# Pooled scores on four quarters of the PE array, and a pair of transposes in one go

## The chip, the cores and the metric

The kernel runs on one core of a Trainium2 chip. The metric is the device time of one execution in microseconds. The kernel before took 961.01 us (median of three runs, 960.36 to 964.61). Of an execution recorded by the hardware profiler there is a trace, and all rows below come from it.

## The reference

Two attentions are added, and the sum goes through a two-layer network. Shapes are fixed: batch 8, 8 heads, 576 positions, head dimension 64, so 4608 tokens of 512 features, and a hidden width of 2048.

```python
q_d, k_d, v_d = (a.reshape(B, H, 144, 4, D).mean(axis=3) for a in (q, k, v))   # pooled by 4
out_up = np.repeat(sm_attn(q_d, k_d, v_d), 4, axis=2)      # softmax attention, 144 x 144 scores a head
scores = where(abs(i - j) < 4, q @ k.T / 8, -1e9)          # local attention, 7 keys a query
out_local = softmax(scores) @ v
x = (out_up + out_local).transpose(0, 2, 1, 3).reshape(4608, 512)
h = x @ w_in
out = maximum(0.01 * h, h) @ w_out
```

(Shortened; both softmaxes subtract the maximum and divide by the sum plus 1e-9.)

## The kernel before, in words

The network is the bulk of PE's work. Its inputs are split into a high and a low part (`xh`, `xl`, weights and `gh`, `gl` likewise), and three products of parts make one. Tokens are worked off in 13 chunks of 256 to 384 columns; chunks 0 and 1 are batch 0, the others batches 1 to 7. For each chunk and each of 16 slices of the hidden width there is an up step (L706, 12 matmuls into a PSUM bank `hp`), an activation (L716, L717 on ACT, L719 on DVE: `gh`, `gl`, three buffers each) and a down step (L746, 12 matmuls into four banks `acc0` to `acc3`). `xh` and `xl` are double buffered by chunk.

The attention prepares x. For batches 1 to 7 the local part is multiplied on POOL (L567, L628) and summed on DVE (L573, L634). `landing` then transposes a piece of it on PE into a bank (L665), adds the widened pooled output (`up`, L652 and L672), and writes `xh` (L678) and `xl` (L680). A chunk's up steps wait for all its landings.

The pooled part is `pooled`, once for each batch and each pair of heads: four units in batch 0 at the start, 28 for the other batches. One unit: the loads of q and k (`qk`) and of v (`vs`); sums over four neighbours on DVE (L345; POOL does it for three of the four units of batch 0); scores on PE (L358): three query groups of 48, fetched as 64 columns, for each of the two heads, with head 0 on partitions 0 to 63 of the array and of the result and head 1 on 64 to 127, all in one bank; the maximum (L366) and its scaling (L367) on DVE; three exponentials with their sums on ACT (L370); the reciprocal on DVE (L373, L374), which frees the bank; the scaling (L382); the pooled v (L387); three transposes into a bank and their copy, twice (L397 on PE, L399 on ACT); the product with v (L409) and its copy to `outd` (L414).

PSUM has eight banks: four `acc`, two `hp`, two `pt`. Until the first chunk is ready, batch 0 may take any of them (`banks`). After that the scores, the transposes and products of `pooled` and the transposes of `landing` share the two `pt` banks.

The order of all instructions is planned when the program is built. Each step is a generator that asks for buffers (`slot`), waits for events and puts operations with an estimated duration (`op`, `pe`, `load`); `Order.run` always takes the operation that can start first by these estimates, and among equals the one of lower rank. Engines work off their queues in the order so written. A holder of a `pt` bank is moved up in rank (`HURRY`). A wait on a bank is thus planned around by the estimate, and held by a semaphore on the chip. All loads are issued on SP's queue.

Of the kernel before, what the change touches and what calls it, by code (L numbers as in the profile page):

```python
# [6 lines left out]
F32 = mybir.dt.float32  # L7
# [6 lines left out]
AF = mybir.ActivationFunctionType  # L14
ALU = mybir.AluOpType
AX = mybir.AxisListType
# [3 lines left out]
FAC = 4  # L20
SD = S // FAC
# [5 lines left out]
SCALE = 1.0 / D ** 0.5  # L27
MAXSEG = 4
SIZES = (4, 5, 6, 6, 6, 6, 6, 6, 6, 6, 6)
QB = 48  # L30
# [6 lines left out]
HEADS = 2  # L37
# [145 lines left out]
def attn_moe(ctx: ExitStack, tc, qkt, vd, qb, kb, vb, vwb, band, identb, w_in, w_out, ident, edge, out):  # L183
    nc = tc.nc

    const = ctx.enter_context(tc.tile_pool(name="const", bufs=1))
    wk = ctx.enter_context(tc.tile_pool(name="wk", bufs=1))
    ps = ctx.enter_context(tc.tile_pool(name="ps", bufs=1, space=PSUM))

    bufs = dict(head=HEADS, qk=1, vs=1, qk_d=2, v_d=1, su_vd=2, su_half=1, su_pd=3, su_ptd=2, st_d=3, pd=2, ptd=1, outd=2, q=1, k=1, v=1, s=3, st_l=3, prod=2, up=1,  # L190
                xloc=2, lst=3, gh=3, gl=3, o=2, hp=2, pt=2, xh0=1, xl0=1, xh1=1, xl1=1, acc0=1, acc1=1, acc2=1, acc3=1,
                su_vw=NC, su_vs=NC, su_pt=2)
    od = Order(bufs)
# [1 line left out]
    def slot(*tags):  # L195
        return (yield ("slot", tags, 0))

    def sb(s, shape, dtype, pool=None):
        tag = s.tag
        return (pool or wk).tile(shape, dtype, name=tag, tag=tag, bufs=bufs[tag])  # L200

    def bank(s):
        return ps.tile([128, 512], F32, name=s.tag, tag=s.tag, bufs=bufs[s.tag])

    def op(eng, n, *after, times=1):
        if eng == "PE":
            dur = n
        else:
            a, k = COST[eng]
            dur = times * a + k * n  # L210
        return (yield ("op", eng, dur, max((0.0,) + after), 0, after))

    def pe(us, *after):
        return (yield ("op", "PE", us, max(after) + SAFE, 0))

    def load(out, in_, size, *after):
        t = yield ("op", "SP", 0.3, max((0.0,) + after), size)
        nc.sync.dma_start(out=out, in_=in_)  # L218
        return t

    def wait(name, n=1):
        return (yield ("wait", name, n))

    id_sb = const.tile([128, 128], F32, name="id_sb")
    edge_sb = const.tile([128, BLK, W], F32, name="edge_sb")
    w_in_v = w_in.rearrange("(c p) (f m) -> p f c m", p=128, m=128 * HALFS)
    w_out_v = w_out.rearrange("(f p) e -> p f e", p=128)
# [1 line left out]
    def fixed():  # L229
        yield from wait(("asked", 0, 0))  # L230
        for dst, src, name, size in ((idb_sb, identb, "idb", 32e3), (band_sb, band, "band", 160e3),
                                     (id_sb, ident, "id", 64e3)):
            od.signal(name, (yield from load(dst, src, size)))

    def edges():
# [51 lines left out]
    outd = {}  # L287
# [3 lines left out]
    def banks(b):  # L291
        return ("pt", "acc3", "acc2", "acc1", "acc0", "hp") if b == 0 and "started" not in od.events else ("pt",)
# [37 lines left out]
    def pooled(b, c, rank, pool=None):  # L330
        sq, sv, qk, vs, tq, tv = yield from fetch(b, c, pool)
        s_qd = yield from slot("qk_d")
        qk_d = sb(s_qd, [128, 2 * SD], F32)
        qkr = qk.rearrange("p a (s r) -> p (a s) r", r=FAC)
        if b < BANDED and (b, c) != (0, 0):
            s = yield from slot("su_half")
            half = sb(s, [128, 2 * SD, 2], F32, pool)
            t = yield from op("POOL", 576, tq, s.t, s_qd.t)
            nc.gpsimd.tensor_tensor(out=half, in0=qkr[:, :, :2], in1=qkr[:, :, 2:], op=ALU.add)
            t = yield from op("POOL", 288, t)  # L340
            nc.gpsimd.tensor_tensor(out=qk_d, in0=half[:, :, 0], in1=half[:, :, 1], op=ALU.add)
            s.free(t)
        else:
            t = yield from op("DVE", 1152, tq, s_qd.t)
            nc.vector.tensor_reduce(out=qk_d, in_=qkr, axis=AX.X, op=ALU.add)  # L345
        if sq:
            if b < BANDED:
                od.spawn(rank, keeper(b, c, sq, t))
            else:
                sq.free(t)  # L350
        s_st, s_pd = (yield from slot("st_d")), (yield from slot("su_pd" if pool else "pd"))
        s_b = yield from slot(*banks(b))
        sc = bank(s_b)
        t = yield from pe(0.9, t, s_b.t)
        for qi in range(3):
            for p in range(2):
                rows = slice(64 * p, 64 * p + 64)
                nc.tensor.matmul(sc[rows, qi * SD:(qi + 1) * SD], qk_d[rows, qi * QB:qi * QB + 64],  # L358
                                 qk_d[rows, SD:2 * SD], start=True, stop=True)
        s_qd.free(t)  # L360
        scv = sc[:, :3 * SD].rearrange("p (a s) -> p a s", a=3)
        st, pd = sb(s_st, [128, 2, 3], F32), sb(s_pd, [128, 3, SD], F32, pool)
        mx, rc = st[:, 0], st[:, 1]
        top, sm = sc[:, 3 * SD:3 * SD + 3], sc[:, 3 * SD + 4:3 * SD + 7]
        t = yield from op("DVE", 440, t, s_st.t, times=3)
        nc.vector.tensor_reduce(out=top, in_=scv, axis=AX.X, op=ALU.max)  # L366
        nc.vector.tensor_scalar(out=mx, in0=top, scalar1=-SCALE / (FAC * FAC), scalar2=None, op0=ALU.mult)  # L367
        t = yield from op("ACT", 432, t, s_pd.t, times=8)
        for qi in range(3):
            nc.scalar.activation(out=pd[:, qi], in_=scv[:, qi], func=AF.Exp, scale=SCALE / (FAC * FAC),  # L370
                                 bias=mx[:, qi:qi + 1], accum_out=sm[:, qi:qi + 1])
        t = yield from op("DVE", 10, t, times=4)
        nc.vector.tensor_scalar(out=rc, in0=sm, scalar1=1e-9, scalar2=float(FAC), op0=ALU.add, op1=ALU.mult)  # L373
        nc.vector.reciprocal(out=rc, in_=rc)  # L374
        s_b.free(t)
        if b < BANDED:
            t = yield from op("POOL", 432, t)
            nc.gpsimd.tensor_tensor(out=pd, in0=pd, in1=rc.unsqueeze(2).to_broadcast([128, 3, SD]), op=ALU.mult)
        else:
            t = yield from op("ACT", 432, t, times=5)  # L380
            for qi in range(3):
                nc.scalar.activation(out=pd[:, qi], in_=pd[:, qi], func=AF.Copy, scale=rc[:, qi:qi + 1])  # L382
        s_st.free(t)
        s_vd = yield from slot("su_vd" if pool else "v_d")
        v_d = sb(s_vd, [72, 2, 2, D], F32, pool)
        td = yield from op("DVE", 1050, tv, s_vd.t)
        nc.vector.tensor_reduce(out=v_d, in_=vs, axis=AX.X, op=ALU.add)  # L387
        if sv:
            sv.free(td)
        s_pt = yield from slot("su_ptd" if pool else "ptd")  # L390
        ptd = sb(s_pt, [72, 2, 2, 3, QB], F32, pool)
        for kc in range(2):
            s_b = yield from slot(*banks(b))
            tp = bank(s_b)
            tt = yield from pe(0.27, t, s_b.t)
            for qi in range(3):
                nc.tensor.transpose(tp[0:72, qi * 128:(qi + 1) * 128], pd[:, qi, kc * 72:kc * 72 + 72], id_sb)  # L397
            te = yield from op("ACT", 288, tt, s_pt.t)
            nc.scalar.copy(out=ptd[:, kc].rearrange("k p a q -> k a p q"),  # L399
                           in_=tp[0:72, :384].rearrange("k (a p q) -> k a p q", a=3, p=2)[:, :, :, :QB])  # L400
            s_b.free(te)
        s_pd.free(tt)
        to = yield from wait(("outd", b))
        s_b = yield from slot(*banks(b))
        av = bank(s_b)
        t = yield from pe(0.68, te, td, s_b.t)
        for p in range(2):
            for kc in range(2):
                nc.tensor.matmul(av[64 * p:64 * p + 64, :SD], v_d[:, p, kc], ptd[:, kc, p],  # L409
                                 start=kc == 0, stop=kc == 1)  # L410
        s_pt.free(t)
        s_vd.free(t)
        t = yield from op("ACT", 144, t, to)
        nc.scalar.copy(out=outd[b][:, c], in_=av[:, :SD])  # L414
        s_b.free(t)
        od.signal(("pooled", b, c), t)
        if b == 0:
            od.signal("su", t)
# [12 lines left out]
    def keeper(b, c, sq, t):  # L431
        sq.free(max(t, (yield from wait(("scored", b, c), 2))))
# [109 lines left out]
    VOFF, n = {}, 0  # L542
# [346 lines left out]
```

## Time and profile before

| | us |
|---|---|
| median of three runs (range) | 961.01 (960.36 to 964.61) |
| the profiled execution | 959.72 |
| its span, first to last instruction | 957.9 |
| PE busy | 932.4 |
| DVE, ACT, POOL busy | 595.2, 415.0, 617.8 |

The busy time of PE is a union of rows: matmuls are pipelined and overlap, so a row is longer than the step from one start to the next. The span is what the trace covers; the execution's own time is a little longer.

### The profile page before, as it was taken

What the parts mean: (1) busy time and instruction counts of PE and PEld (TensorE: products, weight loads), DVE (VectorE), ACT (ScalarE), POOL (GpSimd) and SP (SyncE); (2) the same over time, 40 slices, a digit from 0 to 9 for tenths busy, and PEclk for the clock granted to TensorE, in tenths of its full rate; (3) what the DMA queues carried; (4) which work ended last, traced back from release to release, by engine and by line L of the source; (5) the groups of instructions that cost most, each with busy time, mean ns of one, the idle gap of its engine ahead of it and who ended that gap; (6) DMA issues with size and microseconds to landing.
All of it is one profiled execution on the core that took longest, in us unless ns stands there. A gap on an engine that the chain in (4) does not pass through costs nothing.

```text
span 957.9 us, 16170 instructions
## 1 busy us (share of the span) xinstructions
PE 932.4 (97%) x6282; PEld 894.8 (93%) x6282; DVE 595.2 (62%) x895; ACT 415.0 (43%) x1139; POOL 617.8 (64%) x356
## 2 busy tenths in 40 slices
PE   6799999999999999999999999999999999999997
PEld 5588999899999999999999999899999999999997
DVE  5986678888887776787657774862753753311111
ACT  3774555555545543445324553532513423422211
POOL 3759868777888778986798776884885873100000
PEclk9899999999999999999999999999999999999999
DMA  9755665644554523452424442431231220000000
GB/s 264 241 184 181 214 201 179 189 164 145 188 166 122 190 96 116 131 187 95 135 74 146 159 148 101 140 116 58 92 116 58 91 77 31 34 1 1 34 1 33
DMA packets 63180, 117.31 MB, mean 122 GB/s; under 512 B 4944, under 2 KB 32848, under 8 KB 63104
## 3 DMA queue, kind: packets, MB, share of 16 engines
q1 hardware_dynamic: 63104, 116.29, 38.6%
q8 instruction: 49, 0.80, 0.4%
q14 instruction: 27, 0.22, 0.1%
HBM read 105.65 MB, written 10.62 MB: 121 GB/s over the span
## 4 chain that ended last, share of the span: by engine, by line
PE 77%; POOL 8%; DMA 4%; issue 4%; DVE 4%; ACT 2%; SPq 0%; POOLq 0%; DVEq 0%; ACTq 0%
PE hp L706 35%; PE acc L746 34%; POOL prod L567 4%; POOL prod L628 3%; PE pt L358 2%; DMA k<-in_kb_dram 2%; PE pt L397 2%; PE pt L409 2%; PE pt L665 1%; DMA qk<-in_qkt_dram 1%; DVE s L573 1%; DMA v<-in_w_in_dram 0%; SPq L218 0%; DMA vs<-in_w_out_dram 0%; DVE gl L719 0%
## 5 line engine op out<-in xcount | busy, mean ns | idle before, releaser
L567 POOL TENSOR_TENSOR prod<-q,k 128x1344 f32<-128x1344 f32 (+1 forms) x88 | 266.3, 3027 | 81.3 <-DMA k<-in_kb_dram 55.2
L628 POOL TENSOR_TENSOR prod<-v,s 128x1344 f32<-128x1344 f32 (+1 forms) x88 | 265.6, 3021 | 32.3 <-DVE xloc L634 18.2
L706 PE MATMUL hp<-xh,wih 128*128 128x384 f32 (+2 forms) x832 | 279.9, 336 | 5.8 <-DVE gl L719 5.1
L746 PE MATMUL acc<-gh,woh 128*128 128x384 f32 (+2 forms) x832 | 274.4, 330 | 0.3 <-ACT o L780 0.3
L706 PE MATMUL hp<-xl,wih 128*128 128x384 f32 (+2 forms) x832 | 269.5, 324 | 0.3 <-DVE xl L680 0.3
L706 PE MATMUL hp<-xh,wil 128*128 128x384 f32 (+2 forms) x832 | 269.6, 324 | 0.0
L746 PE MATMUL acc<-gh,wol 128*128 128x384 f32 (+2 forms) x832 | 269.0, 323 | 0.0
L746 PE MATMUL acc<-gl,woh 128*128 128x384 f32 (+2 forms) x832 | 268.9, 323 | 0.0
L719 DVE TENSOR_TENSOR gl<-hp,gh 128x384 fp32r<-128x384 f32 (+2 forms) x208 | 108.5, 522 | 215.7 <-ACT hp L717 215.2
L716 ACT ACTIVATE gh<-hp 128x384 fp32r<-128x384 f32 (+2 forms) x208 | 97.3, 468 | 315.6 <-PE acc L746 307.9
L706 PEld LDWEIGHTS hp<-xh,wih 128*128 128x128 f32 x832 | 156.4, 188 | 15.6 <-DVE gl L719 8.0
L746 PEld LDWEIGHTS acc<-gh,woh 128*128 128x128 f32 x832 | 156.2, 188 | 4.0 <-issue 3.2
L706 PEld LDWEIGHTS hp<-xl,wih 128*128 128x128 f32 x832 | 156.7, 188 | 0.5 <-DVE xl L680 0.5
L706 PEld LDWEIGHTS hp<-xh,wil 128*128 128x128 f32 x832 | 156.4, 188 | 0.0
L746 PEld LDWEIGHTS acc<-gl,woh 128*128 128x128 f32 x832 | 156.3, 188 | 0.0
L746 PEld LDWEIGHTS acc<-gh,wol 128*128 128x128 f32 x832 | 156.2, 188 | 0.0
L573 DVE TENSOR_REDUCE s<-prod 128x21 f32<-128x1344 f32 (+1 forms) x88 | 130.2, 1479 | 27.9 <-POOL prod L567 27.9
L634 DVE TENSOR_REDUCE xloc<-prod 128x192 f32<-128x1344 f32 (+1 forms) x88 | 130.1, 1478 | 22.5 <-POOL prod L628 22.1
L717 ACT ACTIVATE hp<-hp 128x384 f32<-128x384 f32 (+2 forms) x208 | 96.1, 462 | 0.0
L672 DVE TENSOR_TENSOR pt<-pt,up 128x384 f32<-128x384 f32 (+1 forms) x44 | 37.8, 861 | 27.6 <-PE pt L665 22.2
L652 ACT COPY up<-outd 128x576 f32<-128x576 f32 x84 | 52.3, 675 | 0.0
L370 ACT ACTIVATE pd<-pt,st_d 128x144 f32<-128x144 f32 x84 | 32.1, 382 | 46.4 <-DVE st_d L367 35.4
(154 smaller groups left out, 754.3 us busy)
## 6 DMA issues: line engine op xcount, KB each, us to landing
k<-in_kb_dram SPq DMA_DIRECT2D x38, 576.0 KB
v<-in_vb_dram SPq DMA_DIRECT2D x38, 576.0 KB
qk<-in_qkt_dram SPq DMA_DIRECT2D x32, 576.0 KB
vs<-in_vd_dram SPq DMA_DIRECT2D x28, 288.0 KB
q<-in_qb_dram SPq DMA_DIRECT2D x38, 192.0 KB
out_dram<-o SPq DMA_DIRECT2D x36, 192.0 KB
v<-in_w_out_dram SPq DMA_DIRECT2D x4, 512.0 KB
prod<-in_w_out_dram SPq DMA_DIRECT2D x4, 512.0 KB
```

Source lines behind the costliest of these rows:

```text
L370: nc.scalar.activation(out=pd[:, qi], in_=scv[:, qi], func=AF.Exp, scale=SCALE / (FAC * FAC), bias=mx[:, qi:qi + 1], accum_out=sm[:, qi:qi ...
L567: nc.gpsimd.tensor_tensor(out=prv, in0=q[:, p, a - j0:z - j0].unsqueeze(2).to_broadcast([128, n, W, D]), in1=view(k[:, p], (a - j0) * D, [ ...
L573: nc.vector.tensor_reduce(out=s[:, p, a - j0:z - j0], in_=prv, axis=AX.X, op=ALU.add)
L628: nc.gpsimd.tensor_tensor(out=prv, in0=view(v[:, p], a - j0, [[1, n], [nv, D], [1, W]]), in1=s[:, p, a - j0:z - j0].unsqueeze(2).to_broadc ...
L634: nc.vector.tensor_reduce(out=xl_t[:, :n, p], in_=prv, axis=AX.X, op=ALU.add)
L652: nc.scalar.copy(out=up[:, pp], in_=outd[b][:, 2 * u + pp].unsqueeze(2).to_broadcast([128, SD, FAC]))
L672: nc.vector.tensor_tensor(out=xv, in0=xv, in1=upv, op=ALU.add)
L706: nc.tensor.matmul(hp[:, :n], wt[:, c], x[:, c], start=k == 0, stop=k == 3 * NC - 1)
L716: nc.scalar.activation(out=gh[:, :n], in_=hp[:, :n], func=AF.Prelu, alpha=0.01)
L717: nc.scalar.activation(out=hp[:, :n], in_=hp[:, :n], func=AF.Prelu, alpha=0.01)
L719: nc.vector.tensor_tensor(out=gl[:, :n], in0=hp[:, :n], in1=gh[:, :n].bitcast(F32), op=ALU.subtract)
L746: nc.tensor.matmul(acc[:, :n], wt[:, es], g[:, :n], start=f == f0 and j == 0, stop=f == f1 - 1 and j == 2)
```

## The change: the diff

- The scores of query group 1 go to the other two quarters of the array: head 0 writes partitions 64 to 127 and head 1 partitions 0 to 63, into a second bank, `sx`. Groups 0 and 2 stay on the diagonal quarters and lie side by side in the first bank, `sc`.
- The heads of group 1 thus come out in swapped halves. The identity that transposes group 1 is turned to undo it: `id_sb` grows from 128 to 192 columns, and `turned[1]` is its columns 64 to 191.
- Both banks of a unit are asked for together, one unit at a time (`two`, a slot that is given back as soon as both are granted). The maximum becomes two instructions; the exponential of group 1 comes first, and `sx` is given back behind it.
- The six transposes of a unit follow one another into two banks that are held together; the two copies follow.
- The estimates for PE are 0.65 instead of 0.9 (scores) and 0.5 for all six transposes instead of 0.27 for each three.

```diff
-    id_sb = const.tile([128, 128], F32, name="id_sb")
+    id2_sb = const.tile([128, 192], F32, name="id_sb")
+    id_sb = id2_sb[:, :128]
+    turned = [id2_sb[:, 64 * n:64 * n + 128] for n in range(2)]
...
-                                     (id_sb, ident, "id", 64e3)):
+                                     (id2_sb, ident, "id", 96e3)):
...
+        s_two = yield from slot("two")
         s_b = yield from slot(*banks(b))
-        sc = bank(s_b)
-        t = yield from pe(0.9, t, s_b.t)
-        for qi in range(3):
-            for p in range(2):
-                rows = slice(64 * p, 64 * p + 64)
-                nc.tensor.matmul(sc[rows, qi * SD:(qi + 1) * SD], qk_d[rows, qi * QB:qi * QB + 64],
-                                 qk_d[rows, SD:2 * SD], start=True, stop=True)
+        s_x = yield from slot(*banks(b))
+        sc, sx = bank(s_b), bank(s_x)
+        s_two.free(0.0)
+        t = yield from pe(0.65, t, s_b.t, s_x.t)
+        for p, qi in ((0, 0), (1, 0), (0, 1), (1, 1), (0, 2), (1, 2)):
+            rows = slice(64 * p, 64 * p + 64)
+            h = 1 - p if qi == 1 else p
+            dst = sx[:, :SD] if qi == 1 else sc[:, qi // 2 * SD:(qi // 2 + 1) * SD]
+            nc.tensor.matmul(dst[64 * h:64 * h + 64], qk_d[rows, qi * QB:qi * QB + 64], qk_d[rows, SD:2 * SD], start=True, stop=True)
...
-        t = yield from op("DVE", 440, t, s_st.t, times=3)
-        nc.vector.tensor_reduce(out=top, in_=scv, axis=AX.X, op=ALU.max)
+        t = yield from op("DVE", 440, t, s_st.t, times=4)
+        nc.vector.tensor_reduce(out=top[:, 0:3:2], in_=sc[:, :2 * SD].rearrange("p (a s) -> p a s", a=2), axis=AX.X, op=ALU.max)
+        nc.vector.tensor_reduce(out=top[:, 1:2], in_=sx[:, :SD], axis=AX.X, op=ALU.max)
...
-        t = yield from op("ACT", 432, t, s_pd.t, times=8)
-        for qi in range(3):
-            nc.scalar.activation(out=pd[:, qi], in_=scv[:, qi], func=AF.Exp, ...
+        for n_, group in ((1, (1,)), (2, (0, 2))):
+            t = yield from op("ACT", 144 * n_, t, s_pd.t, times=2.7 * n_)
+            for qi in group:
+                nc.scalar.activation(out=pd[:, qi], in_=scs[qi], func=AF.Exp, ...
+            if n_ == 1:
+                s_x.free(t)
...
-        for kc in range(2):
-            s_b = yield from slot(*banks(b))
-            tp = bank(s_b)
-            tt = yield from pe(0.27, t, s_b.t)
+        s_two = yield from slot("two")
+        s_tp = [(yield from slot(*banks(b))), (yield from slot(*banks(b)))]
+        tps = [bank(x) for x in s_tp]
+        s_two.free(0.0)
+        tt = yield from pe(0.5, t, *(x.t for x in s_tp))
+        for kc, tp in enumerate(tps):
             for qi in range(3):
-                nc.tensor.transpose(tp[0:72, ...], pd[:, qi, kc * 72:kc * 72 + 72], id_sb)
-            te = yield from op("ACT", 288, tt, s_pt.t)
+                nc.tensor.transpose(tp[0:72, ...], pd[:, qi, kc * 72:kc * 72 + 72], turned[qi % 2])
+        te = s_pt.t
+        for kc, tp in enumerate(tps):
+            te = yield from op("ACT", 288, tt, te)
             nc.scalar.copy(out=ptd[:, kc] ...
```

## Rows read from the trace of the kernel before

**Rows 1.** The page's engines: busy time, share of the span, instructions.
```profile
PE 932.4 (97%) x6282; PEld 894.8 (93%) x6282; DVE 595.2 (62%) x895; ACT 415.0 (43%) x1139; POOL 617.8 (64%) x356
```
**Rows 2.** Stretches: length, busy (instructions) of each engine, PE clock, DMA share, GB/s.
```profile
372.00:450.00 78.00, 78.00 (x498) 74.04 (x497) 57.33 (x83) 34.94 (x104) 65.10 (x36) 1.00 0.45 145
```
**Rows 3.** PE's waits: releaser, us in total, times, longest.
```profile
PE hp L706 <- DVE gl L719: 5.1, 10, 1.4
```
**Rows 4.** Timeline around chunk 2's first up step: start, us, instruction, [idle before].
```profile
164.20 0.95 PE L358 MATMUL pt<-qk_d 64*64 64x144 f32 x12
...
167.74 0.18 DVE L374 RECIPROCAL st_d<-st_d 128x3 f32<-128x3 f32 x1
...
168.71 0.60 PE L665 MATMUL pt<-id_sb,xloc 128*128 128x128 f32 x4
...
170.77 0.38 PE L706 MATMUL hp<-xh,wih 128*128 128x256 f32 x1 [0.75 <-ACT xh L678]
```
**Rows 5.** Timeline where chunk 3's up steps begin.
```profile
224.91 0.41 DVE L680 TENSOR_TENSOR xl<-pt,xh 128x256 fp32r<-128x256 f32 x1
...
225.71 0.31 PE L706 MATMUL hp<-xh,wih 128*128 128x320 f32 x1
```
**Rows 6.** Timeline of DVE: the last `xl` of chunk 5.
```profile
352.63 0.56 DVE L680 TENSOR_TENSOR xl<-pt,xh 128x384 fp32r<-128x384 f32 x1
```
**Rows 7.** Timeline of PE: the first up step of chunk 5.
```profile
372.61 0.34 PE L706 MATMUL hp<-xh,wih 128*128 128x384 f32 x1
```
**Rows 8.** Stretches, L358 alone: length, busy (passes) of PE and of its loads.
```profile
100.00:169.00 69.00, 4.76 (x60) 3.42 (x60) 1.00 0.60 187
169.00:292.00 123.00, 8.57 (x108) 6.18 (x108) 1.00 0.52 166
292.00:640.00 348.00, 13.34 (x168) 9.58 (x168) 1.00 0.41 131
```
**Rows 9.** Timeline of PE around one block of scores.
```profile
119.09 0.28 PE L746 MATMUL acc<-gl,woh 128*128 128x256 f32 x1
119.21 0.28 PE L746 MATMUL acc<-gh,wol 128*128 128x256 f32 x1
119.42 0.95 PE L358 MATMUL pt<-qk_d 64*64 64x144 f32 x12
...
120.53 0.28 PE L706 MATMUL hp<-xl,wih 128*128 128x256 f32 x1
```
**Rows 10.** Timeline of PE: one block of the product with v.
```profile
305.23 0.72 PE L409 MATMUL pt<-ptd,v_d 72*64 72x144 f32 x8
```
**Rows 11.** Timeline of weight loads, 305.20 to 305.39 us: those begun by then.
```profile
305.23 0.20 PEld L409 LDWEIGHTS pt<-ptd,v_d 72*64 72x64 f32 x4 [0.25 <-issue]
```
**Rows 12.** Timeline of PE around one burst of pooled transposes.
```profile
307.47 0.34 PE L746 MATMUL acc<-gl,woh 128*128 128x384 f32 x1
307.65 0.33 PE L746 MATMUL acc<-gh,wol 128*128 128x384 f32 x1
307.82 0.49 PE L397 MATMUL pt<-id_sb,pd 128*72 128x128 f32 x3
...
308.32 0.34 PE L746 MATMUL acc<-gl,woh 128*128 128x384 f32 x1
```
**Rows 13.** Timeline of PE: two bursts of transposes back to back.
```profile
238.38 0.31 PE L746 MATMUL acc<-gl,woh 128*128 128x320 f32 x1
238.53 0.31 PE L746 MATMUL acc<-gh,wol 128*128 128x320 f32 x1
238.68 0.49 PE L397 MATMUL pt<-id_sb,pd 128*72 128x128 f32 x3
239.00 0.49 PE L665 MATMUL pt<-id_sb,xloc 128*128 128x128 f32 x3
...
239.48 0.30 PE L706 MATMUL hp<-xl,wih 128*128 128x320 f32 x1
```
**Rows 14.** Groups of DVE by form: count, busy us, mean ns, idle before.
```profile
L366 DVE TENSOR_REDUCE pt<-pt 128x3 f32<-128x432 f32 x28 | 17.2, 613 | 14.9 <-PE pt L358 14.8
```

More of the change, by code (lines that the diff above doesn't have):

```diff
@@ L188, in attn_moe @@
     ps = ctx.enter_context(tc.tile_pool(name="ps", bufs=1, space=PSUM))
-    bufs = dict(head=HEADS, qk=1, vs=1, qk_d=2, v_d=1, su_vd=2, su_half=1, su_pd=3, su_ptd=2, st_d=3, pd=2, ptd=1, outd=2, q=1, k=1, v=1, s=3, st_l=3, prod=2, up=1,
+    bufs = dict(head=HEADS, qk=1, vs=1, qk_d=2, v_d=1, su_vd=2, su_half=1, su_pd=3, su_ptd=2, st_d=3, pd=2, ptd=1, outd=2, q=1, k=1, v=1, s=3, st_l=3, two=1, prod=2, up=1,
                 xloc=2, lst=3, gh=3, gl=3, o=2, hp=2, pt=2, xh0=1, xl0=1, xh1=1, xl1=1, acc0=1, acc1=1, acc2=1, acc3=1,
@@ L351, in pooled @@
         s_st, s_pd = (yield from slot("st_d")), (yield from slot("su_pd" if pool else "pd"))
+        s_two = yield from slot("two")
         s_b = yield from slot(*banks(b))
-        sc = bank(s_b)
-        t = yield from pe(0.9, t, s_b.t)
-        for qi in range(3):
-            for p in range(2):
-                rows = slice(64 * p, 64 * p + 64)
-                nc.tensor.matmul(sc[rows, qi * SD:(qi + 1) * SD], qk_d[rows, qi * QB:qi * QB + 64],
-                                 qk_d[rows, SD:2 * SD], start=True, stop=True)
+        s_x = yield from slot(*banks(b))
[7 more added lines that the diff above has]
+            nc.tensor.matmul(dst[64 * h:64 * h + 64], qk_d[rows, qi * QB:qi * QB + 64], qk_d[rows, SD:2 * SD], start=True, stop=True)
         s_qd.free(t)
-        scv = sc[:, :3 * SD].rearrange("p (a s) -> p a s", a=3)
+        scs = sc[:, :SD], sx[:, :SD], sc[:, SD:2 * SD]
         st, pd = sb(s_st, [128, 2, 3], F32), sb(s_pd, [128, 3, SD], F32, pool)
@@ L364, in pooled @@
         top, sm = sc[:, 3 * SD:3 * SD + 3], sc[:, 3 * SD + 4:3 * SD + 7]
-        t = yield from op("DVE", 440, t, s_st.t, times=3)
-        nc.vector.tensor_reduce(out=top, in_=scv, axis=AX.X, op=ALU.max)
+        t = yield from op("DVE", 440, t, s_st.t, times=4)
+        nc.vector.tensor_reduce(out=top[:, 0:3:2], in_=sc[:, :2 * SD].rearrange("p (a s) -> p a s", a=2), axis=AX.X, op=ALU.max)
+        nc.vector.tensor_reduce(out=top[:, 1:2], in_=sx[:, :SD], axis=AX.X, op=ALU.max)
         nc.vector.tensor_scalar(out=mx, in0=top, scalar1=-SCALE / (FAC * FAC), scalar2=None, op0=ALU.mult)
-        t = yield from op("ACT", 432, t, s_pd.t, times=8)
-        for qi in range(3):
-            nc.scalar.activation(out=pd[:, qi], in_=scv[:, qi], func=AF.Exp, scale=SCALE / (FAC * FAC),
-                                 bias=mx[:, qi:qi + 1], accum_out=sm[:, qi:qi + 1])
+        for n_, group in ((1, (1,)), (2, (0, 2))):
+            t = yield from op("ACT", 144 * n_, t, s_pd.t, times=2.7 * n_)
+            for qi in group:
+                nc.scalar.activation(out=pd[:, qi], in_=scs[qi], func=AF.Exp, scale=SCALE / (FAC * FAC),
+                                     bias=mx[:, qi:qi + 1], accum_out=sm[:, qi:qi + 1])
+            if n_ == 1:
+                s_x.free(t)
         t = yield from op("DVE", 10, t, times=4)
@@ L391, in pooled @@
         ptd = sb(s_pt, [72, 2, 2, 3, QB], F32, pool)
-        for kc in range(2):
-            s_b = yield from slot(*banks(b))
-            tp = bank(s_b)
-            tt = yield from pe(0.27, t, s_b.t)
+        s_two = yield from slot("two")
[4 more added lines that the diff above has]
+        for kc, tp in enumerate(tps):
             for qi in range(3):
-                nc.tensor.transpose(tp[0:72, qi * 128:(qi + 1) * 128], pd[:, qi, kc * 72:kc * 72 + 72], id_sb)
-            te = yield from op("ACT", 288, tt, s_pt.t)
+                nc.tensor.transpose(tp[0:72, qi * 128:(qi + 1) * 128], pd[:, qi, kc * 72:kc * 72 + 72], turned[qi % 2])
+        te = s_pt.t
+        for kc, tp in enumerate(tps):
+            te = yield from op("ACT", 288, tt, te)
             nc.scalar.copy(out=ptd[:, kc].rearrange("k p a q -> k a p q"),
                            in_=tp[0:72, :384].rearrange("k (a p q) -> k a p q", a=3, p=2)[:, :, :, :QB])
-            s_b.free(te)
+            s_tp[kc].free(te)
         s_pd.free(tt)
@@ L859 @@
     identb = ident.astype(ml_dtypes.bfloat16)
+    ident = np.concatenate([ident, ident[:, :64]], axis=1)
     pos = halo.reshape(NBLK, HALO)[:, np.arange(BLK)[:, None] + np.arange(W)[None, :]] - (FAC - 1)
```

## The prediction

> **What bounds the kernel now.** I read four views, from the whole to the block. The first is the page's line of engines: PE is busy for 932.4 of 957.9 us, and DVE, ACT and POOL for two thirds of that or less [rows 1]. The reader is to see that one engine has hardly any idle time, and that the others cannot be the bound on average. An average hides stages, so the second view is the table of stretches: from 372 to 450 us PE is busy for all 78.00 us at a granted clock of 1.00, the 2.4 GHz level [rows 2]. The third is the list of PE's waits: the largest behind the start-up is the wait for gl, 5.1 us over ten times [rows 3]. So from about 100 us on, time taken out of PE's stream comes off the end, unless x for the next chunk is late.
>
> That "unless" is the fourth view, the timeline at the changes of chunk. Chunk 2 is at the edge: PE had run out of down projections, took the last landing's transposes at 168.71 and then stood 0.75 us for xh [rows 4]. The last xl of chunk 3 ends at 225.32 and its first matmul starts at 225.71 [rows 5]. For chunk 5 the last xl is done at 353.19, 19 us before the first use at 372.61 [rows 6, 7]. From there on supply is well ahead.
>
> **What the change touches.** The pooled scores run 336 passes after the start-up, 12 for each pair of heads, so 28 units: 60 passes (5 units) before 169 us, 108 (9) from there to 292, 168 (14) after [rows 8]. (Each of the six matmuls on fp32 appears as two passes.)
>
> **Scores over four quarters.** A block now: the dense matmul ahead of it starts at 119.21, the second one behind it at 120.53. Dense matmuls of this width start 0.12 us apart, so two of them would have taken 0.24 of the 1.32 us and the block costs 1.08 us [rows 9]. The row itself says 12 passes in 0.95 us; with 0.28 us for the last pass the starts spread over 0.67 us. Twelve passes one after another don't fit in that with 0.28 us each unless they overlap. The nearest thing to the new block is the block of L409: eight passes of the same 144 columns, in 0.72 us [rows 10]. Both are read alike: the two diagonal quarters, or the two column halves, run side by side, so 12 passes are six rounds and eight are four. Two rounds are then 0.95 - 0.72 = 0.23 us, and by the starts (0.67 over five steps) up to 0.27. Six rounds of 0.12 leave some 0.35 of the 1.08 us for entering and leaving the mode with small tiles, and that stays.
>
> The new order gives queries 0 and 2 to the two diagonal quarters (four passes each) and query 1 to the two others (two passes each). If all four run side by side, the longest quarter has four passes: four rounds instead of six. That saves 0.23 to 0.25 us a unit; I take 0.24. No row shows two row halves that write the same PSUM partitions at once, which is new here. The bounds: nothing saved, if the halves take turns, and 0.27 at the most, as four passes on one quarter cannot be shortened. I take the upper region, because L409's block has both its column halves fed from the same 72 rows and still fits in four rounds, and L358's has two row halves at once: each half of the new pattern is there.
>
> In L409's block the first four weight loads lie within 0.20 us, two for either column half, so the second pair is loaded while the first pair of matmuls (0.28 us or more each) is in flight on the same rows [rows 10, 11]. The Trainium skill (TensorE: Matmul & The Clock Gate, "Part 3: Packing small matmuls — row/col tiling") says that LDWEIGHTS overlaps with in-flight matmuls "only when row_grp differs"; by it the quarters that share a row half could not hide each other's loads, and the scores would save little or nothing. The trace disagrees on L409's rows; it has no such row for four quarters.
>
> **Both transposes together.** A burst of three costs 307.65 to 308.32 less two dense steps of 0.17, so 0.33 us [rows 12]. If entering and leaving cost something, two bursts in a row would be cheaper than two apart. They aren't: three pooled and three landing transposes back to back take 238.53 to 239.48 less two steps of 0.15, so 0.65 us, twice 0.33 [rows 13]. A burst has no fixed part worth saving: at most 0.01 us a unit, 0.2 us in all. The turned identity has the same 128x128 shape, so the same price.
>
> **What is added.** DVE's maximum is one instruction of 0.61 us [rows 14] and becomes two; the second costs between nothing and another 0.61, I take 0.1 for its fixed part: 28 times that is 3 us on an engine that is idle for over 360 us [rows 1]. ACT runs the same exponentials in another order. These, POOL and DVE hide behind PE; without that cover, in the chain of the pooled units of batch 1 ahead of chunk 2, the 0.1 stands against 0.24 saved on PE and the dense matmuls that no longer stand between the two bursts of transposes (three steps of 0.12, 0.35 [rows 9], where there are three), so that chain gets no longer. The identity is 32 KB larger; at the 145 GB/s of a busy stretch [rows 2] that is 0.2 us on SP's queue at the start, ahead of the weights, between nothing and 0.2; I take nothing, since the four start-up units save up to 4 x 0.24 there.
>
> The added wait is for two banks at once, at the scores and at the transposes, out of the two that pt has. PE runs its queue in order, so behind such a wait stand all projections. The order is planned, and a bank that is expected late moves the block, not the queue; what the wait really hits is landings, which need the same banks. A score unit keeps its bank from 164.20 to the reciprocal's end at 167.92, 3.7 us [rows 4]. From chunk 5 on a landing can wait that long several times over [rows 6, 7]. Before it, that is the last rival.
>
> **The sum.** Of 28 units, five lie before 169 us; PE then waits for chunk 2 anyway, so their 1.2 us are gone into that wait. 23 x 0.24 = 5.5, with the transposes 5.7 us. From the profiled execution's own 959.72 (its span of 957.9 and 1.8 around it): 954.0. The median of the runs is 1.3 us above that execution, so 955.3.
>
> **Rivals.** (1) The quarters take turns: the scores stay at six rounds, and only 0.2 us are left: 960.8. For it: no row shows four at once. Against it: both halves of the pattern are shown. 0.12.
> (2) Supply eats more: all 14 units before 292 us gain nothing, since chunks 3 and 4 arrive when they did and PE waits. 14 x 0.24 + 0.2 = 3.6: 957.4. For it: chunk 3's 0.4 us of margin [rows 5]. Against it: gh has three buffers, so up to three steps of down projections (12 matmuls of 0.12 us, 1.4 us a step [rows 9]) can fill such a wait. 0.16.
> (3) The other side: the double hold delays landings. Its place is the last landing of chunks 2, 3 and 4, and its price one hold of 3.7 us each. One late landing still leaves a gain of 2.0; from the second on the gain is gone (955.3 + 7.4 = 962.7), with three it is 966.4. For it: at 168.71 four landing transposes of two pieces take both banks, just behind a score unit's release [rows 4]. Against it: the score unit already stands in their way now, and the second bank is given back after the first exponential. 0.14, half of it with three.
> (4) The shorter chain of batch 1 lets chunk 2 come earlier: four units by 0.24 + 0.35 are 2.4 us more: 952.9. For it: that chain ends in the widened copies that the last landing adds. Against it: transfers and ACT's queue lie between its links. 0.10.
> The forecast has the other 0.48, with 953 to 957.5 as its own range, since the planner orders everything anew and a block more or less beside another is worth some tenths.
>
> **How the numbers follow.** A change under 0.5% (4.8 us) cannot be told from none here: faster means under 956.2, slower over 965.8. Faster: two thirds of the forecast's 0.48, all of (4), a third of (2), and a little for a better order: 0.50. Slower: the three-hold part of (3) and a start-up order that turns out worse: 0.10. The rest, 0.40, lies between. The range takes in (1), (2), (4) and the two-hold case, 950.5 to 963.5.
>
> **What would show it.** The scores' row: 12 passes in about 0.70 us instead of 0.95, and a block that costs 0.84. If it still reads 0.95, rival 1. The transposes as one row of six in about 0.82 us. PE's waits unchanged but for those on xh and xl near 170, 225 and 290 us: several us there mean rival 2 or 3; a landing whose transposes come a hold later tells which. If the span falls by far more than the scores' rows do, the transposes or the order gave what I cost at nothing, and the prediction is wrong in that step.

## The result, and the profile after

| | us | runs | ratio to before (95% interval) |
|---|---|---|---|
| before | 960.42 | 20 | |
| after | 967.09 (962.01 to 970.89) | 20 | 1.0063 (1.0051 to 1.0074) |

The change makes the kernel 0.6% slower. The forecast was 955.3, and the time lies above its range. The profiled execution of the kernel after took 964.09 us with a span of 962.3, 4.4 more than before; it is one of the quicker of the twenty.

The page's line of engines of the kernel after:

```profile
PE 928.1 (96%) x6282; PEld 891.0 (93%) x6282; DVE 606.2 (63%) x927; ACT 413.5 (43%) x1139; POOL 616.2 (64%) x356
```

PE is busy for 4.3 us less than before [rows 1], and the span is 4.4 us longer. So PE's work did shrink, and PE stands idle more. First the blocks, as the timeline of PE shows them (start, us, instruction), one of scores and one of transposes:

```profile
127.92 0.31 PE L719 MATMUL hp<-xh,wil 128*128 128x320 f32 x1
128.15 0.71 PE L364 MATMUL pt<-qk_d 64*64 64x144 f32 x12
...
129.04 0.31 PE L719 MATMUL hp<-xl,wih 128*128 128x320 f32 x1
...
134.91 0.31 PE L719 MATMUL hp<-xh,wil 128*128 128x320 f32 x1
135.06 0.82 PE L408 MATMUL pt<-id_sb,pd 128*72 128x128 f32 x6
...
135.87 0.31 PE L719 MATMUL hp<-xl,wih 128*128 128x320 f32 x1
```

Twelve passes take 0.71 us instead of 0.95, and the block costs 1.12 less two dense steps of 0.15, 0.82 us instead of 1.08 [rows 9]. Six transposes cost 0.96 less 0.30, 0.66 us, as two bursts did [rows 12]. All 28 units together, in the table of stretches for L364 alone (busy us and passes of PE first):

```profile
100.00:1000.00 900.00, 20.22 (x336) 12.42 (x336) 0.99 0.34 107
```

That is 20.22 us against 26.67 in [rows 8] (4.76, 8.57 and 13.34), 0.23 us a unit.

So where is the loss? In the same kind of table over all engines (length, then busy us and instructions of PE, PEld, DVE, ACT and POOL, the granted clock, DMA) one stretch stands out. Before:

```profile
110.00:190.00 80.00, 78.05 (x637) 73.35 (x636) 65.43 (x113) 44.13 (x138) 61.39 (x39) 1.00 0.62 194
```

After:

```profile
110.00:190.00 80.00, 70.34 (x542) 65.06 (x541) 68.54 (x111) 38.07 (x118) 59.82 (x38) 0.96 0.57 182
```

In the same 80 us PE gets 95 passes fewer through, is idle for 7.7 us more, and its granted clock is not full all the time. A pass is 0.12 to 0.15 us apart from the next there, so this stretch alone is worth over 10 us. The two rows also say what it is made of: 7.7 us are pauses, and 0.04 of 80 us, some 3 us by this estimate, is the lower clock. Up to 110 us both kernels are level (854 and 863 passes).

PE's waits behind 60 us in the kernel after, longest first (us, times, longest):

```profile
PE hp L719 <- DVE gl L732: 5.7, 6, 2.2
PE pt L364 <- DVE xl L693: 3.4, 1, 3.4
PE pt L508 <- DVE xl L541: 1.5, 1, 1.5
PE acc L759 <- DVE o L784: 1.4, 2, 0.9
```

In the kernel before, the wait for gl between 100 and 130 us is this:

```profile
PE hp L706 <- DVE gl L719: 0.3, 1, 0.3
```

The wait of 2.2 us lies at 116.8, the one of 3.4 at 174.8. For the first, DVE's timeline in the kernel after:

```profile
113.26 1.39 DVE L272 SCALAR_TENSOR_TENSOR vs<-vs,head 128x512 int32<-128x512 int32 x1
114.57 2.64 DVE L272 SCALAR_TENSOR_TENSOR up<-up,head 128x512 int32<-128x512 int32 x1
117.13 0.41 DVE L280 CAST woh<-vs 128x512 fp32r<-128x512 f32 x1
117.47 1.07 DVE L586 TENSOR_REDUCE s<-prod 128x14 f32<-128x896 f32 x1
118.49 0.42 DVE L732 TENSOR_TENSOR gl<-hp,gh 128x256 fp32r<-128x256 f32 x1
```

and POOL's and ACT's at the same time:

```profile
114.06 2.61 POOL L580 TENSOR_TENSOR prod<-q,k 128x896 f32<-128x896 f32 x1
...
117.24 0.66 ACT L283 CAST wih<-up 128x512 fp32r<-128x512 f32 x1 [3.25 <-DVE up L272]
...
118.09 0.37 ACT L730 ACTIVATE hp<-hp 128x256 f32<-128x256 f32 x1
```

gl, for which PE waits, stands behind the weight conversions twice: in DVE's own queue, and through ACT, whose activations (L729, L730) come behind a cast (L283) that waits 3.25 us for the second L272. L730 ends at 118.46, and gl begins at 118.49. That L272 takes 2.64 us, though the shortest of its kind takes 0.65, so it alone is 2 us late against a wait of 2.16: it ends 0.5 us behind the POOL instruction beside which it began. The Trainium skill (SBUF — State Buffer, "Who interferes with whom") says that a DVE instruction with two SBUF inputs contends with a GpSimd instruction that reads SBUF; L272 has two, and these rows agree. What matters here: how long a conversion takes depends on which POOL instruction the order puts beside it, and the planner's estimates know nothing of that.

For the second wait, PE's timeline of the kernel after:

```profile
174.51 0.28 PE L719 MATMUL hp<-xh,wil 128*128 128x256 f32 x1
178.21 1.09 PE L364 MATMUL pt<-qk_d 64*64 64x144 f32 x12 [3.42 <-DVE xl L693]
179.23 0.58 PE L719 MATMUL hp<-xh,wih 128*128 128x256 f32 x1
```

DVE's:

```profile
174.76 1.13 DVE L685 TENSOR_TENSOR pt<-pt,up 128x256 f32<-128x256 f32 x2 [0.23 <-ACT up L665]
176.38 1.35 DVE L347 TENSOR_REDUCE qk_d<-qk 128x288 f32<-128x1152 f32 x1 [0.49 <-DMA qk<-in_qkt_dram]
177.65 0.74 DVE L693 TENSOR_TENSOR xl<-pt,xh 128x256 fp32r<-128x256 f32 x2
```

and the table of stretches for that wait and what follows:

```profile
174.80:178.20 3.40, 0.00 (x0) 0.02 (x1) 2.91 (x5) 1.89 (x4) 3.23 (x3) 1.00 1.04 312
178.20:182.00 3.80, 3.79 (x25) 3.31 (x26) 3.23 (x6) 0.66 (x2) 3.78 (x3) 0.55 0.69 225
```

Two landings hold both `pt` banks until their xl (L693) is written. DVE does that only behind a pooled sum (L347) whose load it has to wait for. The scores need both banks, and with them PE's whole queue stands. But that sum is also what these scores read, their own qk_d (the sum before it, at 159.13, belongs to the block at 163.07). It ends at 177.73, and the scores begin at 178.21. So the banks can account for 0.5 of the 3.42 us at most; for the rest the block stands in PE's queue ahead of its own load. Behind the pause the clock is granted at 0.55 of full speed, the 1.2 GHz level for nearly all of the 3.8 us, so PE loses some 1.7 us more (an estimate: 0.45 of 3.8). Behind the first pause it is alike:

```profile
120.30:123.80 3.50, 3.50 (x20) 3.50 (x19) 2.95 (x2) 0.00 (x0) 2.41 (x2) 0.52 0.18 72
```

Chunk 2's up steps begin only at 173.8 and are held up at once.

### The profile page after: what moved, and what is told of

Its sections match the earlier page's. It is cut to its first block, busy times and chain, and to the rows that moved or that the text cites. A ratio compares the mean times of both kernels' runs of the same rounds, so it can differ in the third digit from the quotient of the medians.

```text
span 962.3 us, 16215 instructions
## 1 busy us (share of the span) xinstructions
PE 928.1 (96%) x6282; PEld 891.0 (93%) x6282; DVE 606.2 (63%) x927; ACT 413.5 (43%) x1139; POOL 616.2 (64%) x356
## 4 chain that ended last, share of the span: by engine, by line
PE 83%; DMA 5%; DVE 5%; POOL 2%; issue 2%; ACT 1%; SPq 0%; DVEq 0%; POOLq 0%; ACTq 0%
PE acc L759 38%; PE hp L719 38%; PE pt L364 2%; PE pt L408 2%; PE pt L422 2%; PE pt L678 1%; DMA k<-in_w_in_dram 1%; POOL prod L580 1%; DMA v<-in_vb_dram 1%; DMA su_vs<-in_vd_dram 1%; DMA o<-out_dram 1%; DMA k<-in_kb_dram 1%; DVE prod L272 1%; DVE xloc L647 1%; POOL wol L285 1%
## 5 line engine op out<-in xcount | busy, mean ns | idle before, releaser
L729 ACT ACTIVATE gh<-hp 128x384 fp32r<-128x384 f32 (+2 forms) x208 | 97.4, 468 | 321.6 <-PE acc L759 311.4
L730 ACT ACTIVATE hp<-hp 128x384 f32<-128x384 f32 (+2 forms) x208 | 96.2, 462 | 0.0
```

Source lines behind the costliest of these rows:

```text
L729: nc.scalar.activation(out=gh[:, :n], in_=hp[:, :n], func=AF.Prelu, alpha=0.01)
L730: nc.scalar.activation(out=hp[:, :n], in_=hp[:, :n], func=AF.Prelu, alpha=0.01)
```

## The experiments

Three theories. A: the loss comes from batch 0, planned anew. B: it comes from waiting for two banks at once. C, formed after the first four runs: the loss is that of a newly planned order in the first 190 us, whatever the reason it was planned anew. The kernels hold both codes and choose by batch; the widened identity is in all of them. Their line numbers differ from those of the kernel after: L761 is the up step, L373 the new scores, L439 the paired transposes, L720 the transposes of a landing, L733 xh, L735 xl. Where neither code is used and no estimate differs, the traces show the orders of PE, DVE and POOL of before, but for two nearby passes on PE that change places at 24 us in most of these kernels (e7 otherwise agrees up to 217 us, e12 up to 223).

| run | median us | ratio (95% interval) |
|---|---|---|
| e1 batch 0 only | 968.79 | 1.0090 (1.0071 to 1.0108) |
| e2 from batch 1 | 966.57 | 1.0067 (1.0042 to 1.0092) |
| e3 scores only | 971.33 | 1.0119 (1.0094 to 1.0144) |
| e4 transposes only | 970.05 | 1.0104 (1.0087 to 1.0121) |
| e5 estimates down | 969.22 | 1.0097 (1.0078 to 1.0117) |
| e6 estimates up | 970.82 | 1.0118 (1.0095 to 1.0140) |
| e7 from batch 3 | 956.19 | 0.9970 (0.9954 to 0.9986) |
| e8 from batch 3, scores | 955.82 | 0.9955 (0.9939 to 0.9972) |
| e9 from batch 2, scores | 961.99 | 1.0029 (1.0011 to 1.0047) |
| e10 from batch 1, scores | 966.30 | 1.0074 (1.0050 to 1.0098) |
| e11 as e10, kept estimates | 965.00 | 1.0051 (1.0031 to 1.0071) |
| e12 estimates late | 959.89 | 0.9998 (0.9985 to 1.0011) |

(The kernel before took 959.8 to 960.4 us beside them. The ratios are not taken from these medians; the ratios of the medians differ from them by some 0.1% at most.)

**Parts of the change (e1 to e4).**

```diff
-        (new scores and new transposes in every unit)
+        if NEW_S(b): ...   # the new scores, else those of before
+        if NEW_T(b): ...   # the paired transposes, else those of before
+# e1: b < 1 for both    e2: b >= 1 for both    e3: all b, False    e4: False, all b
```

> The new scores and paired transposes in the four units of batch 0 alone; the 28 later units as before. Theory A (the loss comes from the start: the planner orders batch 0 anew, weights are converted later, and PE stands near 112 to 119 us): the whole loss is here, a ratio of 1.006 to 1.010, because the 28 later units don't give their 0.24 us each back. Theory B (the loss comes from the later units, which wait for two pt banks at once): 0.998 to 1.002, as before.

> The new code in the 28 units of batches 1 to 7, batch 0 as before, so that every engine's order is as before up to some 115 us. Theory A: the gain that was forecast comes out, 0.993 to 0.996 (28 x 0.24 = 6.7 us less what the wait for chunk 2 eats). Theory B: still 1.003 to 1.008, with a PE wait of some us in front of the scores near 165 to 185 us.

> Scores over four quarters in all units, the transposes in two bursts with one bank each as before (with the turned identity). If the pair of transposes is what holds the banks (a form of theory B): 0.994 to 0.998. If the scores' second bank is: 1.004 to 1.008. Theory A says nothing definite, since the start is planned anew again: the PE rows of the later units still save 0.24 us each.

> The pair of transposes in all units, the scores as before in one bank. By the prediction's own row (a burst has no fixed cost) nothing is saved on PE: 0.999 to 1.002 if the two banks harm nobody, 1.003 to 1.010 under theory B if holding both for the transposes delays landings.

Each part alone is slower than before, and none is clearly faster than the whole. e1 lies in theory A's range, e2 in B's, e3 above every range given and e4 just above B's. Neither theory holds both e1 and e2: batch 0 alone costs 0.9% without a later unit touched, and the later units alone cost 0.7% with batch 0 as before. The table of stretches of e1:

```profile
110.00:190.00 80.00, 71.74 (x554) 66.77 (x554) 66.05 (x103) 38.98 (x121) 57.05 (x37) 0.96 0.58 181
```

The same stretch as in the kernel after, with nearly the same figures, and no score unit that needs two banks in it. In e2 the waits behind 60 us are others, but lie in the same stretch:

```profile
PE pt L439 <- ACT pd L421: 3.2, 1, 3.2
PE hp L761 <- DVE gl L774: 2.9, 8, 0.6
PE pt L373 <- DVE xl L735: 2.8, 1, 2.8
```

The last of them stands in front of the scores at 178.52. Their own sum ends at 176.61 here, so up to 1.9 us of it can be the two banks: in this order theory B may have a part.

**Other estimates, same instructions (e5, e6).** Now nothing is changed but the order.

```diff
-        t = yield from pe(0.9, t, s_b.t)      # scores
+        t = yield from pe(0.65, t, s_b.t)     # e6: 1.08
...
-            tt = yield from pe(0.27, t, s_b.t)  # transposes
+            tt = yield from pe(0.25, t, s_b.t)  # e6: 0.33
```

> The code of before with the same instructions; only the planner's estimates for PE are other: 0.65 instead of 0.9 for the scores, 0.25 instead of 0.27 for each burst of transposes. So only the order differs, from the start on. Theory C (the loss is that of a newly planned order in the first 250 us, whatever the reason it was planned anew; the order of before is a favourable one among many): 1.004 to 1.012. Theory B (waits for two banks): 0.999 to 1.002, since nothing waits for two banks here.

> The same the other way: the estimates raised to what the trace shows, 1.08 for the scores and 0.33 for a burst. Theory C: again slower, 1.003 to 1.012, though the estimates are now the truer ones. Theory B: 0.999 to 1.002. If lowered estimates are slower and truer ones faster, the cause is the estimate itself.

Both are 1.0 to 1.2% slower, more than the change itself, with no wait for two banks and no instruction altered. Truer estimates (e6) are no better than lowered ones. So the order alone can bring a loss of this size, and theory B is not needed for it; that the double wait cost nothing in the other orders is not shown by this. PE's longest waits behind 60 us in e5:

```profile
PE hp L761 <- DVE gl L774: 5.7, 7, 2.2
PE hp L761 <- ACT xh L733: 2.7, 1, 2.7
PE pt L720 <- DVE xl L735: 1.6, 1, 1.6
```

The last two lie at the first use of chunk 2, between 174.2 and 179.6. e5 in the table of stretches:

```profile
110.00:190.00 80.00, 70.25 (x550) 64.87 (x548) 67.07 (x105) 39.90 (x123) 56.81 (x36) 0.98 0.57 183
```

The conversions on DVE are one sign of what another order does. Busy time of that line (L272) alone, from 60 to 130 us, in the table of stretches (busy us and count of DVE behind the length), before:

```profile
60.00:130.00 70.00, 17.54 (x17) 1.00 0.62 195
```

in the kernel after:

```profile
60.00:130.00 70.00, 21.43 (x18) 0.98 0.59 187
```

and in e5:

```profile
60.00:130.00 70.00, 21.64 (x18) 1.00 0.58 186
```

One instruction more in the stretch, and 4 us more of DVE's time. e1 has 21.58 us for 18, e6 19.56 for 19 and e7, which gains, 17.73 for 17. How much of the loss this makes is not shown.

e6 loses in several places: by 110 us it is 30 passes behind, by 190 us another 24. The stretch from 20 to 48 us of e6:

```profile
20.00:48.00 28.00, 23.43 (x199) 16.07 (x200) 23.17 (x43) 18.44 (x51) 18.25 (x16) 0.57 0.82 256
```

PE is at the lower clock for some 24 of the 28 us (by the mean of 0.57) and gets 199 passes through. That alone is not decisive: e8 below has a clock of 0.66 there and is the fastest.

**The change where there is room (e7, e8).**

```diff
+# e7: b >= 3 for scores and transposes    e8: b >= 3 for the scores alone
```

> The whole change in batches 3 to 7 alone (20 units); every order is as before up to some 218 us. Theory C with the saving per unit as the trace of the changed kernel shows it: 20 x 0.24 = 4.8 us less, 0.994 to 0.997. Theory B: 0.999 to 1.004, since the later units wait for two banks like the earlier ones.

> As the run from batch 3 on, but only the scores; the transposes stay in two bursts with one bank each. Theory C: the same gain, 0.994 to 0.997, as the paired transposes save nothing on PE. If holding two banks for the transposes costs something of its own, this one is faster than the run with both by 1 us or more.

Now it gains: 0.3 and 0.45%, 3.6 and 3.9 us by the medians, where 4.8 was expected. The critical stretch of e7 is that of before:

```profile
110.00:190.00 80.00, 78.12 (x639) 73.38 (x637) 66.34 (x114) 43.81 (x137) 61.38 (x38) 1.00 0.61 193
```

Its 20 units hold two banks as in the kernel after, and no wait for xl in front of a score block is left in its trace. e8 is not slower than e7, so pairing the transposes brings nothing; that e8 is faster is within both intervals.

**How early it may begin (e9 to e11).**

```diff
+# e9: scores alone, b >= 2    e10: scores alone, b >= 1    e11: as e10, and
-        t = yield from pe(0.65, t, s_b.t, s_x.t)
+        t = yield from pe(0.9, t, s_b.t, s_x.t)
-            t = yield from op("ACT", 144 * n_, t, s_pd.t, times=2.7 * n_)
+        t = yield from op("ACT", 432, t, s_pd.t, times=8)   # and DVE times=3
```

> Scores alone, in batches 2 to 7 (24 units); orders as before up to some 164 us, so only the stretch at the first use of chunk 2 (164 to 185 us) is planned anew beside the run from batch 3 on. Theory C, with that stretch as one of the places where a new order loses: 0.999 to 1.006, with PE waits of some us or a drop of the clock there. If the loss lies only ahead of 164 us (start and weights): 24 x 0.24 = 5.8 us less, 0.993 to 0.996.

> Scores alone, in batches 1 to 7 (28 units), batch 0 as before. Against the run of the whole change in the same batches (1.0067) this tells what the paired transposes add: theory C says nothing of their own, so somewhere between 0.997 and 1.008, as the new order falls out; if the pair's double hold is a cost of its own, 0.994 to 0.997.

> The same instructions as the run before (scores alone, batches 1 to 7), but the planner is told the estimates of before (0.9 for PE, one operation of 432 for the exponentials, three reductions' fixed parts), so the order stays as before up to some 119 us and differs from the run before only as an order. Theory C: the two differ by 2 us or more from each other with equal work. If the order doesn't matter, they agree within 1.5 us.

e9 differs from e8 in four units and in the orders from 164 us on, and the gain of 0.45% becomes a loss of 0.3%. So the first use of chunk 2 is itself a place where such a change loses. In e9 the four units and the order change together; e5, whose order alone is new, waits there too. Before, in the table of stretches:

```profile
164.00:171.00 7.00, 6.25 (x53) 5.60 (x48) 5.41 (x12) 4.82 (x15) 6.97 (x4) 1.00 0.32 109
171.00:181.20 10.20, 9.29 (x79) 8.56 (x80) 8.88 (x14) 4.23 (x13) 6.25 (x5) 1.00 0.87 273
```

and e9:

```profile
164.00:171.00 7.00, 5.22 (x36) 4.02 (x35) 5.81 (x14) 3.96 (x13) 5.52 (x4) 1.00 0.58 177
171.00:181.20 10.20, 9.00 (x50) 7.53 (x49) 7.74 (x14) 3.45 (x10) 6.99 (x6) 0.50 0.86 284
```

In e9 PE waits three times for about 1 us each from 167.7 to 172.4 and is at half clock from 171.0 to 181.2. Busy for nearly as long as before, it gets 50 passes through instead of 79. Most of the loss in this stretch is the clock, not the pauses themselves. e10 and e11 have equal work and two orders. They lie 1.3 us apart, within the 1.5 that would say that the order doesn't matter; this pair doesn't support theory C.

**A new order behind the tight stretch (e12).**

```diff
-        t = yield from pe(0.9, t, s_b.t)
+        t = yield from pe(0.9 if b < 3 else 1.0, t, s_b.t)
```

> The code of before with the same instructions; only the estimate for the scores of batches 3 to 7 is 1.0 instead of 0.9, so that the orders are as before up to some 230 us and planned anew behind that. Theory C in its narrow form (only the stretch ahead of some 185 us is so tight that a new order loses): 0.998 to 1.002. If any newly planned order loses, wherever it begins: 1.004 to 1.012, as the two runs whose estimates differ from the start on.

No difference. The one order tried that has the instructions of before and is new from some 230 us on costs nothing; one that reaches into the first 190 us cost 0.3 to 1.2% in each of the ten kernels that had one, the kernel after among them.

Where the time goes, from the traces: start of the last down matmul of a chunk (or of its first half), in us, less that of before (110.2, 235.9, 615.6, 952.6):

| | chunk 1, first half | chunk 2 | chunk 7 | last chunk |
|---|---|---|---|---|
| after | -1.1 | +9.9 | +5.5 | +4.4 |
| e1 batch 0 only | -0.3 | +11.0 | +10.9 | +10.1 |
| e5 estimates down | -0.6 | +4.0 | +7.9 | +8.8 |
| e6 estimates up | +4.0 | +9.1 | +9.2 | +10.1 |
| e7 from batch 3 | -0.2 | -3.6 | -4.3 | -4.4 |
| e8 from batch 3, scores | +0.3 | -0.2 | -3.7 | -3.5 |
| e9 from batch 2, scores | -0.9 | +5.4 | +2.6 | +2.4 |

The kernel after loses 11 us between the first two columns and wins 5.5 back behind them. e1 loses as much there and wins 0.9 back, since its later units are the old ones. The difference of the two behind chunk 2, 4.6 us, agrees with the saving that was forecast: the kernel after has 19 units there, and 19 x 0.24 is 4.6. A single mark is not that exact, since it also moves with how the order mixes up and down steps.

## Why the prediction was wrong

- **What bounds the kernel.** That PE bounds it from 100 us on was right from some 230 us on, where e7 and e8 gain and e12 loses nothing, and too generous for 110 to 190. In that stretch PE was busy because the order of before has each conversion, load and landing in time; e5 and e6, with the same instructions, don't keep it busy.
- **Scores over four quarters.** Right: four rounds, 0.24 us a unit forecast, 0.23 measured over 28 units. Rival 1 falls: twelve passes fit in 0.71 us. The first eight weight loads of that block begin while its first four passes, on the same two row halves, are still running (timeline of PEld and PE up to 128.30):

```profile
128.15 0.21 PEld L364 LDWEIGHTS pt<-qk_d 64*64 64x64 f32 x8 [0.20 <-issue]
...
128.15 0.35 PE L364 MATMUL pt<-qk_d 64*64 64x144 f32 x4
```

  The Trainium skill (TensorE: Matmul & The Clock Gate, "Part 3: Packing small matmuls — row/col tiling") says that loads overlap with matmuls in flight only on other rows; these rows disagree, for four quarters too.
- **Both transposes together.** Right: 0.66 us for six, nothing saved; and e8, which leaves the pair out, is no slower than e7.
- **What is added on DVE.** Mis-sized, but e7 and e8 gain in spite of it. The two maxima, by form (count, busy us, mean ns):

```profile
L371 DVE TENSOR_REDUCE pt<-pt 128x2 f32<-128x288 f32 x30 | 13.9, 464 | 19.4 <-PE pt L364 19.0
L372 DVE TENSOR_REDUCE pt<-pt 128x1 f32<-128x144 f32 x28 | 8.9, 316 | 1.0
```

  0.46 + 0.32 - 0.61 = 0.17 us a unit, where 0.1 was taken.
- **The added wait.** "A bank that is expected late moves the block, not the queue" was wrong: a block can stand in the queue ahead of what it needs, and the queue stood for 3.42 us at 174.8. Of that the two banks explain 0.5 us at most, and of 2.8 us in e2 up to 1.9; the rest is the place that the order gave to the block. e5 and e6 lose more without any wait for two banks, so it is not what the loss needs.
- **The step that failed** is the sentence under the rivals: "the planner orders everything anew and a block more or less beside another is worth some tenths". Measured, the new order was worth 11 us between 110 and 236 us, and by e5 and e6 an order alone can cost 9.5 to 11 us in all. I added up what the changed instructions cost and took the rest of the order as given, though [rows 4] showed chunk 2 without margin and the kernel's text shows that each estimate decides the order of all that follows. The start-up, the conversions and the loads were costed at nothing because their instructions are unchanged; their places are not. "A start-up order that turns out worse" stood in the text and comes nearest, but it had only what the three-hold part of (3) left of 0.10, and the loss lies behind the start-up: at 110 us the kernel after is level.
- **Rivals.** (3) had the side and one of the places (chunk 2) right, but its mechanism, landings held up by a double hold, is not what the runs show: in the kernel after a block of scores waits behind landings, not the other way round, and e1, e5 and e6 have no double hold in that stretch. (2) asked whether chunks 3 and 4 eat the gain, and stays open: e7 gains 3.6 us by the medians and 4.4 in its trace; of its 20 units five begin before 292 us, so 15 x 0.24 = 3.6 would be left if these gained nothing, and 4.8 if all gain. (4) did not happen: chunk 2's up steps begin at 173.83 instead of 169.06.
- **What stays open.** Why the order of before is better than the others tried is shown only in part: conversions beside POOL work, loads that land later than planned, and the lower clock behind pauses. In the kernel after the pauses are the larger part (7.7 us against some 3 us of clock between 110 and 190), but what share each cause of a pause has was not taken apart. In e2, e3, e4 and e9 to e11 the new units and the new order come together, and e10 and e11 do not part them. Whether another early order would be as good as that of before was not tried; the orders of the kernel after, e1 and e5 are alike in their waits at 112 and 117 us, so they are fewer than they look.

Two versions beat both kernels, e7 and e8. The simpler is e8: scores over four quarters in batches 3 to 7, all else as before, 0.9955 (0.9939 to 0.9972).

## What to carry to other kernels

Where a planner writes the order, run the old instructions with one estimate changed before you cost a change: here that alone cost 1.0 to 1.2%, more than the change could bring. Then apply the change only where the profile shows margin, so that the order of the tight stretch stays as it is. And look at a stretch by the work that gets through (passes), not by PE's busy time: at half clock PE looks just as busy.

## What the runs showed of the hardware that was not expected

- Four quarters of the array, two of them on the same rows and two on the same PSUM partitions in two banks, run 12 passes in 0.71 us where the two diagonal quarters take 0.95.
- The same DVE instruction on SBUF operands (L272, 32 times in the kernel after) took from 0.65 to 2.67 us, and what decided was which engine began first. Those that began while a POOL instruction ran ended 0.55 to 0.59 us behind it; those that began alone, or just ahead of a POOL instruction, took 0.65 to 0.70.
- Two pauses of 0.8 and 1.0 us that ended at 168.5 and 170.7 were followed by half clock from 171.0 to 181.2 (e9; a third pause, of 1.2 us, lies within it), while in the kernel before PE also paused for 0.75 us at 170 us [rows 4] and kept the full clock. Over the twenty executions of the kernel after, the mean granted clock lies between 0.994 (964.09 us) and 0.984 (967.59 and 970.89 us); the longer executions tend to have the lower one.
